# A fused attention and two-MLP kernel on one core: the first keys fetched and split per head, and three early steps issued behind the first scores

## The chip, the cores and the metric

One core of a Trainium2 chip. The metric is device microseconds of one execution; a comparison uses the median of several executions of either kernel. Engines are named as in the profile: PE (TensorE, matrix products; PEld its weight loads), DVE (VectorE), ACT (ScalarE), POOL (GpSimd), SP (SyncE, which here issues nearly all DMAs). SPq is SP's instruction queue.

## What is computed

```python
# attention, 2 x 8 heads, 576 rows, head size 64: only the 32 largest scores of a row count
scores = scale * q @ k.T
kth = np.partition(scores, -32, axis=-1)[..., -32:-31]
scores = np.where(scores >= kth, scores, -1e9)
x = softmax(scores) @ v                      # -> 1152 tokens x 512
# first MLP (float64 weights, 512 x 1536 twice and 1536 x 512)
xn = x / sqrt(mean(x * x) + 1e-6) * rms_g
x = (silu(xn @ w_gate) * (xn @ w_val)) @ w_out
# second MLP, routed: each token to the best of 8 experts, 512 x 1024 and 1024 x 512 each
out = gate_w * (relu(x @ w1[e]) @ w2[e])
```

## The kernel before, in words

The work runs in 36 attention pairs (9 tiles of 128 tokens, 4 pairs of heads each). A pair `p` is a query block, two heads `i`; `scores(p, i)` makes a row of 576 scores in two halves of 288 columns, each from two products on PE (rounded and residual part of the query), which ACT copies out (line 319). DVE then folds the two halves into larger and smaller ones (lines 324, 325) and `topk_folded` finds the 32 largest by rounds of "eight largest" (MAX8, lines 367, 376, 378, 379) and "strike them out" (line 373).

Before the products, keys and queries are split into a rounded part (ACT copy, lines 271 and 295) and a residual (a subtraction, lines 272 and 296, on DVE for pair 0 and on POOL later). The keys of two heads come as two DMAs of 64 partitions, one per partition half (`fetch_k`, line 266); the two partition halves are the two parts that one product contracts over, so a head's product needs both DMAs.

At the same time the weights of the first MLP are converted from float64 (`convert_all`): 12 units of 1 MB and 12 of 0.5 MB are fetched by `fetch` (line 137, always on SP), and `bits` makes 32-bit words of one: ACT rounds the low words (line 167), DVE joins them with the high ones (line 168) and sets the exponent (line 169). A gram product (line 193) and a few small steps find a power-of-two scale per block, whose last factor is the largest square of `rms_g` (lines 243 and `top`, lines 178 to 182), and `split` (lines 238 to 241) writes two half-precision parts. Only when all blocks are split can `moe1` of tile 0 start (lines 498 and 523), in which PE works off the first MLP tile by tile beside the attention of later tiles. The last 150 us are the routed MLP.

The order on each engine isn't written out: the code gives an order of issue (a list of slots, `at`, with priorities by `ahead`), and a scheduler then fixes one static order per engine from its own estimate of the times. Within an engine's order nothing overtakes. A new construct in the changed kernel, `tc.issue_after(x)`, keeps the instructions in its block from being placed ahead of `x`. Each DMA reports on one of eight landing semaphores, handed out in turn, and an issue waits until the previous DMA on its semaphore has landed.

The first instructions at the top of the program (lines 648 to 663): query 0, keys of pair 0, first weight unit, `rms_g`, query 1, keys of pair 1, two more units, then the splits and scores of pair 0, then the splits of pair 1.

Of the kernel before, what the change touches and what calls it, by code (L numbers as in the profile page):

```python
# [1 line left out]

# [6 lines left out]
F32 = mybir.dt.float32  # L9
# [4 lines left out]
U32 = mybir.dt.uint32  # L14
U8 = mybir.dt.uint8
AF = mybir.ActivationFunctionType
OP = mybir.AluOpType
PSUM = bass.MemoryType.PSUM

P = 128  # L20
B, H, S, D = 2, 8, 576, 64
N = B * S
DM = H * D
# [4 lines left out]
HALF = S // 2  # L28
KC = DM // P
# [14 lines left out]
LOW = 0.937  # L44


def tile_topk_attention__then__moe__then__moe_routed(
    tc: tile.TileContext,
    q_l, k_l, v_l, w_gate, w_val, w_out, rms_g, r_gate, w1, w2, capacity, out,
):  # L50
    args = (q_l, k_l, v_l, *(a.bitcast(I32) for a in (w_gate, w_val, w_out)), rms_g, r_gate, w1, w2, int(capacity), out)
    general, held, store = whole(tc, *args, False)
    with tc.If(general > W):
        whole(tc, *args, True)
        for to, _, _ in held[1:]:
            tc.nc.gpsimd.memset(to, int(NOWHERE))
    for x in held[1:]:
        store(*x)
    held[0].release()
# [3 lines left out]
def whole(  # L63
# [3 lines left out]
    nc = tc.nc  # L67
# [18 lines left out]
    gk = const.tile([P, KC], F32, name="gk")  # L86
    st = const.tile([P, 70], F32, name="st")
    inv, rinv, ga, g2 = st[:, 0:7], st[:, 7:14], st[:, 14:38].rearrange("p (b c) -> p b c", c=KC), st[:, 38:46]
# [18 lines left out]
    pm = tc.alloc_tile_pool(name="pm", bufs=3, space=PSUM)  # L107
# [10 lines left out]
    def staged(b, c):  # L118

        return 4 * b + 4 + c  # L120
# [1 line left out]
    def final(b, c):  # L122
        return 4 * b + c

    def fetch():
        n = coming[0]
        coming[0] += 1
        b, c, g = UNITS[n]
        r = slice(c * P, (c + g) * P)
        src = w_out[r, :] if b == 6 else (w_gate, w_val)[b % 2][r, (b // 2) * 2 * DM:(b // 2 + 1) * 2 * DM]  # L130
        if (b, c) in PLACE:
            at = PLACE[b, c]
            raw = wbig[:, at:at + 2 * g, :].bitcast(I32).rearrange("p (a two) f -> p a (two f)", two=2)
        else:
            raw = att.tile([P, g, 2 * DM], I32, name="wraw", bufs=4)
        wraw[n] = raw.rearrange("p a (f w) -> p a f w", w=2)
        nc.sync.dma_start(raw, src.rearrange("(a p) f -> p a f", p=P))

    def pow2_below_rsqrt(out, back, x, by, t):

# [12 lines left out]
    def convert_all():  # L153

        due = {}
        n = 0

        def later(k, f, *a):
            due.setdefault(n + k, []).append((f, a))

        def bits(n):
            b, c, g = UNITS[n]
            raw = wraw.pop(n)
            j = staged(b, c)
            a = wbig[:, j:j + g, :].bitcast(I32)
            low = raw[:, :, :, 0]
            nc.scalar.activation(low.bitcast(F32), low.bitcast(U32), AF.Copy, scale=-LOW * 2.0 ** -51, bias=-2.0)
            nc.vector.scalar_tensor_tensor(a, raw[:, :, :, 1], 3, low, op0=OP.logical_shift_left, op1=OP.bitwise_or)  # L168
            nc.vector.scalar_tensor_tensor(a, raw[:, :, :, 1], 0x3fffffff, a, op0=OP.bitwise_or, op1=OP.bitwise_and)  # L169
            while coming[0] < len(UNITS) and coming[0] <= n + (3, 4)[n >= 9]:  # L170
                fetch()
            if c + g == (NF1 if b == 6 else KC):
                later(1, gram, b)

        def top(out, x, row):

            m = route.tile([P, 8], F32, name="m8")
            nc.vector.max(m, x)
            d = mx.tile([P, ROW], F32, name="yd").bitcast(BF16)[:, :P]
            nc.scalar.activation(d, ident, AF.Copy, scale=m[:, 0:1])  # L180
            nc.tensor.matmul(row, ones16, d, start=True, stop=True)
            nc.vector.max(out, row)
# [57 lines left out]
            nc.tensor.matmul(t, negated, half(i, 0), start=False, stop=True)  # L240
            nc.scalar.activation(half(i, 1), t, AF.Copy)

        nc.vector.tensor_tensor(g2[:, 0:KC], gk, gk, op=OP.mult)
        top(g2, g2, pm.tile([P, DM], F32, name="pm")[:, :P])
        start, k = {}, 0
        for i, u in enumerate(UNITS):
            start[k] = i
# [1 line left out]
        while n < k or due:  # L249
            if n in start:  # L250
                bits(start[n])
            for f, a in due.pop(n, []):
                f(*a)
            n += 1
            yield
# [3 lines left out]

    raw = {}  # L260

    def fetch_k(b, hp):
        row = 12 * (hp % 2) if b == 0 else NW
        raw["k", b, hp] = wbig[:, row:row + 3, :].rearrange("p a f -> p (a f)")[:, :2 * S].rearrange("p (i s) -> p i s", i=2)
        for half in range(2):
            nc.sync.dma_start(raw["k", b, hp][64 * half:64 * half + 64], k_l[b, :, 2 * hp:2 * hp + 2, :])

    def split_k(b, hp, eng=nc.gpsimd):
        x = raw.pop(("k", b, hp))
        st = att.tile([P, 2, S], F32R, name="kst", bufs=6)  # L270
        nc.scalar.activation(st, x, AF.Copy)
        eng.tensor_tensor(st[64:], x[64:], st[64:].bitcast(F32), op=OP.subtract)
        kst[b, hp] = st

    def load_v(b, hp):
# [15 lines left out]
    def split_q(p, eng=nc.gpsimd):  # L291
        x = raw.pop(("q", p))
        qh[p] = att.tile([P, 2, P], F32R, name="qh", bufs=3)
        ql[p] = att.tile([P, 2, P], F32R, name="ql", bufs=3)
        nc.scalar.activation(qh[p], x, AF.Copy)
        eng.tensor_tensor(ql[p], x, qh[p].bitcast(F32), op=OP.subtract)

    def spans_of(t):
        lo, hi = t * P, t * P + P
        if hi <= S:  # L300
            return [(0, 0, P)]
        if lo >= S:
            return [(1, 0, P)]
        return [(0, 0, S - lo), (1, S - lo, P)]

    s_sb = {}

    hi, lo = {}, {}

    def scores(p, i):  # L310
        t, hp = divmod(p, 4)
        s = att.tile([P, S], F32, name="s", bufs=4)
        for c in range(2):
            sp = ps.tile([P, KC, P], F32, name="tp", bufs=3).rearrange("p a b -> p (a b)")[:, :HALF]
            for b, _, c1 in reversed(spans_of(t)):
                for n, x in enumerate((qh[p], ql[p])):
                    nc.tensor.matmul(sp[:c1], x[:, i, :c1], kst[b, hp][:, i, c * HALF:(c + 1) * HALF],  # L317
                                     start=(n == 0), stop=(n == 1))
            nc.scalar.activation(s[:, c * HALF:(c + 1) * HALF], sp, AF.Copy)  # L319
        s_sb[p, i] = s  # L320
        if not exact:
            r = att.tile([P, 2, HALF], F32, name="r", bufs=4)
            hi[p, i], lo[p, i] = r[:, 0], r[:, 1]
            nc.vector.tensor_tensor(hi[p, i], sp, s[:, :HALF], op=OP.max)  # L324
            nc.vector.tensor_tensor(lo[p, i], sp, s[:, :HALF], op=OP.min)  # L325

    def pair_scores(p):
        for i in range(2):
            scores(p, i)
# [317 lines left out]
    SL = 14  # L647
    fetch_q(0)
    fetch_k(0, 0)
    fetch()  # L650
    nc.sync.dma_start(gk, rms_g.rearrange("(c p) -> p c", p=P))
    fetch_q(1)
    fetch_k(0, 1)
    fetch()
    fetch()
    split_q(0, nc.vector)
    split_k(0, 0, nc.vector)
    scores(0, 0)
    scores(0, 1)
    split_q(1)  # L660
    split_k(0, 1)
    fetch_k(0, 2)
    load_v(0, 0)
    at(4, ahead(convert_all(), 300, 1000), 1.0)
    at(4, once(split_k, 0, 2))
    at(4, once(fetch_k, 0, 3))
    at(10, once(split_k, 0, 3))
# [21 lines left out]
    for p in range(NP):  # L689
        t, hp = divmod(p, 4)  # L690
# [343 lines left out]
    top = route.tile([P, 1], I32, name="top", bufs=1)  # L1034
# [76 lines left out]
```

## Time and profile before

| | |
|---|---|
| median of 3 executions | 672.41 us (672.27 to 673.39) |
| profiled execution | 673.78 us, of which the span from first to last instruction 672.0 us |
| busy in the span | PE 88%, DVE 79%, ACT 75%, POOL 54% |
| mean granted clock of PE | 0.97 of full speed |
| DMA | 80.05 MB, 119 GB/s over the span |

All times of the trace count from the start of the span; 1.8 us of the profiled execution lie outside it. A busy PE in this profile is not a PE at its peak, since its products are pipelined. An instruction's duration includes some 0.06 us to 0.1 us in which the next one has already started.

### The profile page before, as it was taken

What the parts mean: (1) busy time and instruction counts of PE and PEld (TensorE: products, weight loads), DVE (VectorE), ACT (ScalarE), POOL (GpSimd) and SP (SyncE); (2) the same over time, 40 slices, a digit from 0 to 9 for tenths busy, and PEclk for the clock granted to TensorE, in tenths of its full rate; (3) what the DMA queues carried; (4) which work ended last, traced back from release to release, by engine and by line L of the source; (5) the groups of instructions that cost most, each with busy time, mean ns of one, the idle gap of its engine ahead of it and who ended that gap; (6) DMA issues with size and microseconds to landing.
All of it is one profiled execution on the core that took longest, in us unless ns stands there. A gap on an engine that the chain in (4) does not pass through costs nothing.

```text
span 672.0 us, 13486 instructions
## 1 busy us (share of the span) xinstructions
PE 589.9 (88%) x4817; PEld 414.1 (62%) x4817; DVE 533.8 (79%) x1489; ACT 503.2 (75%) x978; POOL 364.1 (54%) x499
## 2 busy tenths in 40 slices
PE   1428878899998999999999999999798769999994
PEld 1314455446665667666676666665344669999994
DVE  3989999978899878888989899751647746999961
ACT  3469978996788798797878887876984519998721
POOL 2487554445569699778788796784614000132112
PEclk9999969899999999999999999999898779999998
DMA  8998256923000010001000000009300499999001
GB/s 234 260 349 283 105 195 228 275 52 79 14 13 33 12 48 29 13 10 31 17 25 17 9 25 1 1 19 362 153 1 19 154 193 388 322 349 354 27 22 41
DMA packets 47006, 80.05 MB, mean 119 GB/s; under 512 B 18716, under 2 KB 23324, under 8 KB 46930
## 3 DMA queue, kind: packets, MB, share of 16 engines
q1 hardware_dynamic: 43938, 74.02, 35.0%
q0 software_dynamic: 1792, 4.83, 1.9%
q8 instruction: 39, 0.64, 0.4%
q10 hardware_dynamic: 1200, 0.26, 0.2%
q14 instruction: 37, 0.30, 0.1%
HBM read 64.35 MB, written 12.27 MB: 114 GB/s over the span
## 4 chain that ended last, share of the span: by engine, by line
PE 48%; DVE 14%; ACT 12%; DMA 10%; POOL 7%; issue 6%; SPq 1%; POOLq 0%; ACTq 0%; DVEq 0%
PE pm L498 14%; PE pm L523 9%; PE xps L430 6%; PE acc L905 5%; PE tp L317 4%; PE tp L422 4%; DMA raw<-in_w_dram 3%; DVE split L819 2%; ACT junk L789 2%; DMA vt<-in_v_l_dram 2%; PE pm L238 2%; DVE wbig L168 1%; DVE wbig L169 1%; DMA gk<-in_rms_g_dram 1%; POOL pp L399 1%
## 5 line engine op out<-in xcount | busy, mean ns | idle before, releaser
L498 PE MATMUL pm<-wbig,xn 128*128 128x512 f16 x600 | 148.9, 382 | 0.1
L905 PEld LDWEIGHTS <-split 128*128 128x128 f16 x1728 | 117.9, 101 | 12.1 <-DMA xbT<-xb 5.9
L399 POOL TENSOR_TENSOR pp<-s,pp 128x576 f32<-128x576 f32 x72 | 102.0, 1433 | 18.0 <-ACT pp L398 17.6
L498 PEld LDWEIGHTS <-xn 128*128 128x128 f16 x648 | 62.8, 99 | 59.7 <-issue 2.0
L376 DVE MAX8 m<-r 128x8 f32<-128x288 f32 x216 | 96.2, 452 | 2.4
L373 DVE MATCH_REPLACE8 r<-m,r 128x288 f32<-128x288 f32 x216 | 95.1, 442 | 0.0
L317 PE MATMUL tp<-kst,qh 128*128 128x288 f32 (+1 forms) x160 | 64.4, 410 | 31.7 <-ACT s L319 14.4
L523 PE MATMUL pm<-wbig,hT 128*128 128x512 f16 x324 | 79.3, 386 | 1.6 <-ACT hT L468 1.4
L319 ACT ACTIVATE s<-tp 128x288 f32<-128x288 f32 x144 | 57.2, 416 | 13.4 <-PE tp L317 11.0
L819 DVE SCALAR_TENSOR_TENSOR split<-raw,sc,split 128x2048 f16<-128x2048 f32 (+1 forms) x32 | 65.7, 2078 | 0.1
L317 PEld LDWEIGHTS tp<-kst,qh 128*128 128x128 f32 (+1 forms) x160 | 31.3, 195 | 50.4 <-ACT s L319 21.8
L430 PE MATMUL xps<-pt,vt 128*64 128x128 f32 (+1 forms) x800 | 61.9, 275 | 0.0
L905 PE MATMUL acc<-hE,split 128*128 128x168 f16 (+2 forms) x864 | 59.0, 228 | 3.2 <-ACT junk L789 1.3
L422 PE MATMUL tp<-ident,pp 128*128 128x128 f32 x324 | 57.7, 288 | 4.1 <-DVE r L325 2.4
L905 PE MATMUL acc<-xgT,split 128*128 128x168 f16 (+1 forms) x768 | 59.2, 241 | 1.5 <-DMA xgT<-disp 1.5
L398 ACT ACTIVATE pp<-s,bias 128x576 f32<-128x576 f32 x72 | 52.0, 775 | 9.7 <-POOL bias L381 9.7
L404 ACT ACTIVATE pp<-pp,bias 128x576 f32<-128x576 f32 x72 | 56.9, 793 | 2.7 <-POOL pp L399 2.7
L423 ACT ACTIVATE pt<-tp 128x384 f32<-128x384 f32 x108 | 52.0, 500 | 9.2 <-PE tp L422 7.0
L789 ACT ACTIVATE junk<-raw 128x2048 bf16<-128x2048 f32 (+1 forms) x32 | 54.2, 1692 | 3.9 <-DMA raw<-in_w_dram 3.5
L324 DVE TENSOR_TENSOR r<-tp,s 128x288 f32<-128x288 f32 x72 | 32.5, 451 | 28.7 <-ACT s L319 28.2
L422 PEld LDWEIGHTS tp<-ident,pp 128*128 128x128 f32 x324 | 40.4, 145 | 21.9 <-DVE r L325 3.2
L430 PEld LDWEIGHTS xps<-pt,vt 128*64 128x64 f32 x800 | 44.5, 138 | 12.7 <-issue 11.1
(226 smaller groups left out, 1236.4 us busy)
## 6 DMA issues: line engine op xcount, KB each, us to landing
raw<-in_w_dram SPq DMA_DIRECT2D x28, 1024.0 KB, 9.1
wbig<-in_w_gate_dram SPq DMA_DIRECT2D x6, 1024.0 KB, 6.8
wbig<-in_w_val_dram SPq DMA_DIRECT2D x6, 1024.0 KB, 9.9
wraw<-in_w_out_dram SPq DMA_DIRECT2D x12, 512.0 KB, 5.9
disp<-wraw SPq DMA_DIRECT2D x18, 257.0 KB, 6.9
qraw<-in_q_l_dram SPq DMA_DIRECT2D x72, 64.0 KB, 2.3
wbig<-in_k_l_dram SPq DMA_DIRECT2D x16, 288.0 KB, 4.0
split<-in_w_dram SPq DMA_DIRECT2D x4, 1024.0 KB, 7.9
```

The source lines that it names most:

```text
L317: nc.tensor.matmul(sp[:c1], x[:, i, :c1], kst[b, hp][:, i, c * HALF:(c + 1) * HALF], start=(n == 0), stop=(n == 1))
L319: nc.scalar.activation(s[:, c * HALF:(c + 1) * HALF], sp, AF.Copy)
L373: nc.vector.match_replace(h[i], to[n - 1][:, i], h[i], -3.0e38)
L376: nc.vector.max(to[n][:, i], h[i])
L399: nc.gpsimd.tensor_tensor(w, s[i], w, op=OP.subtract)
L422: nc.tensor.transpose(tp[:, i, :], p2[:, o:o + P], ident)
L430: nc.tensor.matmul(xps[t][rows, hp, c0:c1], v, w, start=(n == 0), stop=(n == 4))
L498: nc.tensor.matmul(a, xn[:, x + c, :], half(i, lo), start=(c == 0 and n == 0), stop=(c == KC - 1 and n == 2))
L523: nc.tensor.matmul(yps, hT[f // KC][:, KC * hi + f % KC, :], half(i, lo), start=(f == 0 and n == 0), stop=(f == NF1 - 1 and n == 2))
L789: nc.scalar.activation(junk, raw[:, g * 2 * BIG // k:(g + 1) * 2 * BIG // k], AF.Square, accum_out=sc[:, 9 + g:10 + g])
L819: nc.vector.scalar_tensor_tensor(lo[:, r], raw[:, r], sc[:, 7:8], hi[:, r], op0=OP.mult, op1=OP.subtract)
L905: nc.tensor.matmul(a, u[:, c, col * P:(col + 1) * P], v[:, c, :a.shape[-1]], start=(c == 0 and n == 0), stop=(c == nk - 1 and n == 2))
```

## The change

Four edits, all in the program's first microseconds; everything else in the code is as before, and the scheduler's order follows from it.

1. The first weight unit is fetched on ACT's queue (`fetch(nc.scalar)`), no longer on SP behind the first keys.
2. The keys of pair 0 are fetched and split head by head: four DMAs of half the columns, two copies on ACT and two subtractions on DVE, each of half the size.
3. Query 1 and keys 1 are split only after the copies of both heads' scores of pair 0 have been placed on ACT; the first unit's rounding on ACT and its joining on DVE (lines 168 and 170 of the changed kernel) likewise stand behind those copies and behind the folds.
4. The square of `rms_g` moves from DVE to POOL (line 246), and its maximum is found behind the first unit's joining.

```diff
-    def fetch():
+    def fetch(eng=nc.sync):
...
-        nc.sync.dma_start(raw, src.rearrange("(a p) f -> p a f", p=P))
+        eng.dma_start(raw, src.rearrange("(a p) f -> p a f", p=P))
...
-            nc.scalar.activation(low.bitcast(F32), low.bitcast(U32), AF.Copy, scale=-LOW * 2.0 ** -51, bias=-2.0)
-            nc.vector.scalar_tensor_tensor(a, raw[:, :, :, 1], 3, low, op0=OP.logical_shift_left, op1=OP.bitwise_or)
+            with tc.issue_after(copied[0, 1].ins) if n == 0 and not exact else nullcontext():
+                nc.scalar.activation(low.bitcast(F32), low.bitcast(U32), AF.Copy, scale=-LOW * 2.0 ** -51, bias=-2.0)
+            with tc.issue_after(folded[0, 1].ins) if n == 0 and not exact else nullcontext():
+                joined.append(nc.vector.scalar_tensor_tensor(a, raw[:, :, :, 1], 3, low, op0=OP.logical_shift_left, op1=OP.bitwise_or))
...
-        nc.vector.tensor_tensor(g2[:, 0:KC], gk, gk, op=OP.mult)
-        top(g2, g2, pm.tile([P, DM], F32, name="pm")[:, :P])
+        def gains():
+            nc.gpsimd.tensor_tensor(g2[:, 0:KC], gk, gk, op=OP.mult)
+            with tc.issue_after(joined[0].ins):
+                top(g2, g2, pm.tile([P, DM], F32, name="pm")[:, :P])
+
+        later(3, gains)
...
+    def heads(b, hp):
+        return (0, 1) if b == 0 and hp == 0 else (slice(0, 2),)
...
-        for half in range(2):
-            nc.sync.dma_start(raw["k", b, hp][64 * half:64 * half + 64], k_l[b, :, 2 * hp:2 * hp + 2, :])
+        for i in heads(b, hp):
+            for half in range(2):
+                nc.sync.dma_start(raw["k", b, hp][64 * half:64 * half + 64, i], k_l[b, :, 2 * hp:2 * hp + 2, :][:, i])
...
-        nc.scalar.activation(st, x, AF.Copy)
-        eng.tensor_tensor(st[64:], x[64:], st[64:].bitcast(F32), op=OP.subtract)
+        for i in heads(b, hp):
+            nc.scalar.activation(st[:, i], x[:, i], AF.Copy)
+            eng.tensor_tensor(st[64:, i], x[64:, i], st[64:, i].bitcast(F32), op=OP.subtract)
...
-    fetch()
+    fetch(nc.scalar)
...
-    split_q(1)
-    split_k(0, 1)
+    with tc.issue_after(copied[0, 1].ins):
+        split_q(1)
+        split_k(0, 1)
```

SP's first DMAs. Before (`qraw` queries, `wbig<-in_k_l_dram` keys, `in_w_gate_dram` and `in_w_val_dram` weight units, `gk` is `rms_g`; DMAHW0 to DMAHW7 are the landing semaphores):

```order
L289 DMA qraw<-in_q_l_dram 64x256 x2
L266 DMA wbig<-in_k_l_dram 64x1152 x2
L137 DMA wbig<-in_w_gate_dram 128x2x1024
L651 DMA gk<-in_rms_g_dram 128x4x1
L289 DMA qraw<-in_q_l_dram 64x256 x2
L266 DMA wbig<-in_k_l_dram 64x1152 [waits DMAHW0_49]
L266 DMA wbig<-in_k_l_dram 64x1152 [waits DMAHW1_49]
L137 DMA wbig<-in_w_gate_dram 128x2x1024 [waits DMAHW2_49]
L137 DMA wbig<-in_w_val_dram 128x2x1024 [waits DMAHW3_49]
L266 DMA wbig<-in_k_l_dram 64x1152 [waits DMAHW4_49,Activation_49]
```

And now:

```order
L300 DMA qraw<-in_q_l_dram 64x256 x2
L276 DMA wbig<-in_k_l_dram 64x576 x4
L662 DMA gk<-in_rms_g_dram 128x4x1
L300 DMA qraw<-in_q_l_dram 64x256 [waits DMAHW0_49]
L300 DMA qraw<-in_q_l_dram 64x256 [waits DMAHW1_49]
L276 DMA wbig<-in_k_l_dram 64x1152 [waits DMAHW2_49]
L276 DMA wbig<-in_k_l_dram 64x1152 [waits DMAHW3_49]
L137 DMA wbig<-in_w_gate_dram 128x2x1024 [waits DMAHW4_49]
L137 DMA wbig<-in_w_val_dram 128x2x1024 [waits DMAHW5_49]
L276 DMA wbig<-in_k_l_dram 64x1152 [waits DMAHW6_49,Activation_49]
```

The first weight unit is gone from SP, and the second query's first DMA now waits on DMAHW0, which the first weight unit (on ACT's queue) now reports on; before, that unit reported on DMAHW4, and the third pair's keys waited for it.

ACT's first instructions. Before (`kst` split keys, `qh` split query, `yd` belongs to the maximum of `rms_g`, `s` scores):

```order
L295 ACTIVATE qh_121<-qraw_107 128x256 [waits DMAHW0_49]
L271 ACTIVATE kst_125<-wbig_87 128x1152 [waits DMAHW3_49,DMAHW2_49]
L167 ACTIVATE wbig_87<-wbig_87 128x1024 [waits DMAHW4_49]
L295 ACTIVATE qh_152<-qraw_114 128x256 [waits DMAHW7_49,DMAHW6_49]
L180 ACTIVATE yd_184<-ident_64,m8_182 128x128 [waits DVE_49,Pool_49]
L319 ACTIVATE s_128<-tp_129 128x288 [waits PE_49]
L319 ACTIVATE s_128<-tp_133 128x288 [waits PE_49]
L319 ACTIVATE s_140<-tp_141 128x288 [waits PE_49]
L271 ACTIVATE kst_156<-wbig_87 128x1152 [waits DMAHW1_49,DMAHW0_49]
```

And now:

```order
L137 DMA wbig_87<-in_w_gate_dram 128x2x1024
L306 ACT_TABLE_LOAD [waits DMAHW2_49]
L306 ACTIVATE qh_123<-qraw_107 128x256 [waits DMAHW1_49]
L282 ACTIVATE kst_127<-wbig_87 128x576 [waits DMAHW4_49,DMAHW3_49]
L282 ACTIVATE kst_127<-wbig_87 128x576 [waits DMAHW6_49,DMAHW5_49]
L330 ACTIVATE s_132<-tp_133 128x288 [waits PE_49]
...
L330 ACTIVATE s_144<-tp_149 128x288 [waits PE_49]
L306 ACTIVATE qh_156<-qraw_116 128x256 [waits DMAHW1_49,DMAHW0_49]
L282 ACTIVATE kst_160<-wbig_87 128x1152 [waits DMAHW3_49,DMAHW2_49]
L168 ACTIVATE wbig_87<-wbig_87 128x1024
L168 ACTIVATE wbig_87<-wbig_87 128x1024 [waits DMAHW4_49]
L182 ACTIVATE yd_224<-ident_64,m8_222 128x128 [waits DVE_49]
```

The score copies (four, two of them shown) no longer stand behind the first unit's rounding; that rounding now stands behind the copy of the second pair's keys.

DVE's first work after the constants. Before:

```order
L272 TENSOR_TENSOR kst<-wbig,kst 64x1152
L243 TENSOR_TENSOR st<-gk 128x4
L178 MAX m_182<-st 128x8
L168 SCALAR_TENSOR_TENSOR wbig<-wbig 128x1024
L182 MAX st<-pm 128x8
L324 TENSOR_TENSOR r<-tp,s 128x288
L325 TENSOR_TENSOR r<-tp,s 128x288
L169 SCALAR_TENSOR_TENSOR wbig<-wbig 128x1024
L367 MAX m<-r 128x8
```

And now:

```order
L283 TENSOR_TENSOR kst<-wbig,kst 64x576 x2
L335 TENSOR_TENSOR r<-tp,s 128x288
L336 TENSOR_TENSOR r<-tp,s 128x288
L378 MAX m<-r 128x8
...
L384 MATCH_REPLACE r<-m,r 128x288 x2
L170 SCALAR_TENSOR_TENSOR wbig<-wbig 128x1024
L180 MAX m_222<-st 128x8
L387 MAX m<-r 128x8 x2
L170 SCALAR_TENSOR_TENSOR wbig<-wbig 128x1024
L171 SCALAR_TENSOR_TENSOR wbig<-wbig 128x1024
```

Ten instructions of pair 0's scores (six in the gap) now come ahead of the first unit's joining, and the second unit's joining comes ahead of the first's exponent.

## Rows read from the trace of the kernel before

**Rows 1.** The page: engines' busy us; one group: busy us, mean ns | idle before.

```profile
PE 589.9 (88%) x4817; PEld 414.1 (62%) x4817; DVE 533.8 (79%) x1489; ACT 503.2 (75%) x978; POOL 364.1 (54%) x499
...
L319 ACT ACTIVATE s<-tp 128x288 f32<-128x288 f32 x144 | 57.2, 416 | 13.4 <-PE tp L317 11.0
```

**Rows 2.** Busy time by stretches: length, engines (instructions), granted PE clock, DMA share, GB/s.

```profile
100.00:110.00 10.00, 9.14 (x66) 5.82 (x65) 9.95 (x33) 10.00 (x23) 4.86 (x12) 1.00 0.37 120
...
140.00:150.00 10.00, 9.51 (x56) 5.09 (x55) 6.09 (x19) 10.00 (x25) 4.24 (x7) 1.00 0.27 69
...
300.00:350.00 50.00, 49.92 (x353) 32.39 (x351) 45.12 (x155) 40.10 (x96) 39.90 (x60) 1.00 0.07 20
```

**Rows 3.** Timeline of the first 20 us: start, us, instruction, idle before and its releaser.

```profile
0.73 1.22 SPq L289 DMA_DIRECT2D qraw<-in_q_l_dram  x2
...
1.99 1.24 SPq L266 DMA_DIRECT2D wbig<-in_k_l_dram  x2
...
3.26 0.59 SPq L137 DMA_DIRECT2D wbig<-in_w_gate_dram  x1
...
7.11 1.16 ACT L271 ACTIVATE kst<-wbig 128x1152 fp32r<-128x1152 f32 x1 [1.72 <-DMA wbig<-in_k_l_dram]
...
8.30 1.35 DVE L272 TENSOR_TENSOR kst<-wbig,kst 64x1152 fp32r<-64x1152 f32 x1 [2.46 <-ACT kst L271]
...
9.71 0.61 PE L317 MATMUL tp<-kst,qh 128*128 128x288 f32 x1 [9.71 <-DVE kst L272]
...
12.70 1.10 ACT L167 ACTIVATE wbig<-wbig 128x1024 f32<-128x1024 uint32 x1 [4.43 <-DMA wbig<-in_w_gate_dram]
...
13.08 0.16 DVE L243 TENSOR_TENSOR st<-gk 128x4 f32<-128x4 f32 x1 [3.43 <-DMA gk<-in_rms_g_dram]
...
13.83 1.23 DVE L168 SCALAR_TENSOR_TENSOR wbig<-wbig 128x1024 int32<-128x1024 int32 x1 [0.38 <-ACT wbig L167]
...
15.18 0.44 DVE L324 TENSOR_TENSOR r<-tp,s 128x288 f32<-128x288 f32 x1
15.54 0.45 DVE L325 TENSOR_TENSOR r<-tp,s 128x288 f32<-128x288 f32 x1
...
16.03 1.16 ACT L271 ACTIVATE kst<-wbig 128x1152 fp32r<-128x1152 f32 x1 [0.74 <-DMA wbig<-in_k_l_dram]
...
17.32 2.65 POOL L272 TENSOR_TENSOR kst<-wbig,kst 64x1152 fp32r<-64x1152 f32 x1 [1.67 <-ACT kst L271]
...
18.29 1.14 ACT L167 ACTIVATE wbig<-wbig 128x1024 f32<-128x1024 uint32 x1 [0.80 <-DMA wbig<-in_w_gate_dram]
...
19.46 1.59 DVE L168 SCALAR_TENSOR_TENSOR wbig<-wbig 128x1024 int32<-128x1024 int32 x1
...
20.02 0.61 PE L317 MATMUL tp<-kst,qh 128*128 128x288 f32 x1 [4.43 <-POOL kst L272]
```

**Rows 4.** Busy time by stretches of the start; the last two columns are DMA.

```profile
2.00:4.00 2.00, 0.00 (x0) 0.00 (x0) 0.00 (x0) 0.33 (x1) 1.34 (x7) 1.00 0.55 112
4.00:9.00 5.00, 0.00 (x0) 0.00 (x0) 1.12 (x2) 2.54 (x3) 0.00 (x0) 1.00 0.99 290
...
14.00:19.00 5.00, 1.12 (x3) 0.50 (x2) 4.97 (x11) 3.46 (x8) 3.09 (x2) 1.00 1.04 360
```

**Rows 5.** DMAs issued at 0.73, 1.99 and 7.80 us: count, size, us to landing.

```profile
qraw<-in_q_l_dram SPq DMA_DIRECT2D x1, 64.0 KB, 2.2
...
wbig<-in_k_l_dram SPq DMA_DIRECT2D x1, 288.0 KB, 3.8
...
wbig<-in_w_gate_dram SPq DMA_DIRECT2D x1, 1024.0 KB, 10.5
```

**Rows 6.** What SP's queue waited for, first 20 us: total, times, longest.

```profile
SPq L266 <- DMA wbig<-in_w_gate_dram: 3.7, 1, 3.7
```

**Rows 7.** What DVE waited for, first 60 us: total, times, longest.

```profile
DVE st L243 <- DMA gk<-in_rms_g_dram: 3.4, 1, 3.4
...
DVE wbig L168 <- POOL kst L272: 1.5, 1, 1.5
```

More of the change, by code (lines that the diff above doesn't have):

```diff
@@ L1 @@
-from contextlib import ExitStack
+from contextlib import ExitStack, nullcontext
 import concourse.bass as bass
@@ L306, in whole @@
     s_sb = {}
-    hi, lo = {}, {}
+    hi, lo, copied, folded, joined = {}, {}, {}, {}, []
     def scores(p, i):
@@ L318, in scores @@
                                      start=(n == 0), stop=(n == 1))
-            nc.scalar.activation(s[:, c * HALF:(c + 1) * HALF], sp, AF.Copy)
+            copied[p, i] = folded[p, i] = nc.scalar.activation(s[:, c * HALF:(c + 1) * HALF], sp, AF.Copy)
         s_sb[p, i] = s
@@ L324, in scores @@
             nc.vector.tensor_tensor(hi[p, i], sp, s[:, :HALF], op=OP.max)
-            nc.vector.tensor_tensor(lo[p, i], sp, s[:, :HALF], op=OP.min)
+            folded[p, i] = nc.vector.tensor_tensor(lo[p, i], sp, s[:, :HALF], op=OP.min)
     def pair_scores(p):
```

## The prediction

> **What bounds the kernel now.** I read the busy table first, then the busy times by stretch, then the timeline of the first 20 us, and last who waited for whom. Over the span PE is busiest, with 88% against DVE's 79% [rows 1], but that is a mean over stages. At 100 to 110 us DVE is busy 9.95 of 10 us and ACT 10.00; at 140 to 150 us DVE has fallen to 6.09 and ACT has 10.00; from 300 to 350 us PE has 49.92 of 50 [rows 2]. So the weight conversion with the first top-k rounds is DVE's and ACT's stage, and the tiles behind it are PE's. All four edits lie in the first 20 us. A microsecond of DVE saved there can reach the end, since DVE then works without a pause and PE takes over when the conversion is done.
>
> The reader should see two things in the first 20 us. DVE does nothing useful from the end of the key split (8.30 + 1.35 = 9.65) to 13.08, where it waits 3.4 for `rms_g` [rows 3, 7]; the first fold of scores starts only at 15.18, although the first product ran at 9.71, because ACT's score copies stand behind the rounding of the first weight unit, which landed at 12.70 [rows 3]. And the joining of the second unit at 19.46 follows straight on ACT's rounding of it (18.29 + 1.14 = 19.43), which itself waited 0.80 for the landing [rows 3]. At 19.46, then, it's a DMA and not DVE that is late. From 4 to 9 us the DMA engines are busy 0.99 with 290 GB/s, from 14 to 19 us 1.04 with 360 [rows 4].
>
> **What the change does, part by part.**
>
> *First head.* Its keys are half of what pair 0 fetched, 288 KB, and query 0 is two DMAs of 64 KB [rows 5]; beside them the first weight unit (1024 KB) now flows from the start. Without any sharing the head lands as today's first half of the keys does, of the same 288 KB: 1.99 + 3.8 = 5.8 [rows 3, 5]. If it must share so that all 1440 KB (1.47 MB) come first, it is 1.47 MB at 290 GB/s = 5.1 us from 2.0 us, where the first bytes flow: 7.1, and some tenths until the report. I take 7.3, near the upper end, because 290 GB/s was the rate with the engines already full [rows 4]. ACT's copy (1.16) and DVE's subtraction (1.35) fall to a little over half, say 0.65 and 0.75, so the first product starts at about 8.8 rather than 9.71 [rows 3].
>
> *Second head.* 288 KB more is 1.0 us: landing at 8.3, ACT and DVE done by 9.75. The four halves cost some 0.2 us more than the two wholes, in time when both engines were idle.
>
> *Folds.* The copies follow the products at once, so the first fold starts at about 10.2, not 15.18: two products of 0.61 that overlap [rows 3] end at 9.65 or so, a copy takes 0.42 [rows 1], and DVE is free at 9.75. That is 5 us earlier for pair 0. But DVE did other work in that time. What counts is how far DVE is at one point that both orders share: the joining of the second unit. Before it DVE spends 19.46 - 13.08 - 0.38 = 6.0 us [rows 3]. Now: ten instructions of pair 0 at 0.36 from start to start (15.18 to 15.54) to 0.44, say 3.9; the first unit's joining 1.2; the small maximum 0.1; two more of 0.4: again 6.0. The work is the same, so the gain at that point is 19.46 less the new start of the second unit's joining.
>
> *Second pair's keys.* SP's issue of query 1 now waits for the semaphore on which the first unit reports; call its landing W. That such a wait binds is seen today: the third pair's keys waited 3.7 us for this unit [rows 6]. From query 0's issue to the copy of pair 0's keys it took 7.11 - 0.73 = 6.4 [rows 3], and the same four DMAs follow W, so keys 1 land at W + 6.4. Today they were there at 16.03 [rows 3]. W lies between 0.73 + 1.3 (first bytes) + 1.05 MB at 290 GB/s (3.6) = 5.6, and today's whole time from issue to landing, 12.70 - 3.26 = 9.4, from 0.73: 10.2. With the 1.47 MB above it is 7.1 and some tenths: I take 7.7, hence 14.1 for keys 1.
>
> *First unit's rounding.* On ACT it now stands behind the copy of keys 1. That is 14.1 + 1.16, then 1.10: its joining starts at 16.4. DVE, which has its ten instructions done by 14.3 (10.2 + 3.9, and 0.2 of waiting for the second head), stands idle for 2.1 us. After that it is ready for the second unit at 16.4 + 1.2 + 0.1 + 0.8 = 18.5, a microsecond ahead of today.
>
> *Second unit.* SP issues it after W and four issues of 0.6, at 10.1 to 10.2, where it was 7.80. It can land at the earliest when keys 1 are in and 1.05 MB at 360 GB/s has followed, 14.1 + 2.9 = 17.0; if it takes today's 10.5 [rows 5], at 20.7. Both ends are one row away from the case, so I take the middle, 18.8; with rounding of 1.1 the joining starts at 19.9. That is 0.45 later than 19.46.
>
> *Small parts.* The square of `rms_g` leaves DVE (0.16) and lands on POOL, idle there until the key split of pair 1 at 17.32 [rows 3]. If that cover were gone it would delay pair 1 by what it takes. Pair 1's products start at 14.1 + 1.16 + 2.65 = 18.0, not 20.02, but ACT's copies of them stand behind the second unit's rounding, so little of the 2 us gets through.
>
> *Sum.* Against the profiled execution of 673.78 us (span 672.0 and 1.8 outside it; 1.4 above the median of 672.41): DVE +0.45 at the second unit, -0.16 for the square; today's later idle of 1.5 us on DVE, behind POOL's key splits [rows 7], can take up a lag as small as this; pair 0's and pair 1's rounds lie further ahead, worth perhaps 0.5. Together about -0.4: 673.4 for a profiled execution like this one, 672.0 for the median. The head start of 5 us is spent on waiting for the same bytes.
>
> **Rivals.**
>
> *The head start stays (faster).* If the first unit lands near its lower end, W = 5.6, keys 1 are there at 12.0 and the first joining can start at 14.3, without idle time. The second unit lands between 14.9 and 18.5, and its joining starts between 16.5 (DVE's own pace) and 19.6; in the middle, at 17.8, 1.7 us are gained, at best 3.0. That gives 669.4 to 670.7, say 670.2. For it: from 2 to 4 us the engines are busy only 0.55 [rows 4], room that the early unit fills. Against it: the keys want the same engines just then.
>
> *The early unit is in its own way (slower).* It shares the DMA engines with queries and keys, and SP stands still until it has landed. W = 10.2 gives keys 1 at 16.6, the first joining at 18.9, the second unit between 19.5 and 23.1 and its joining at 22.4: 2.9 us late, of which DVE's later idle of 1.5 may hide some. That is 673.8 to 675.3, say 674.6. By this working the new joining starts at W + 12.2, so the change breaks even at W = 7.3, and loses more than 0.2% above W = 8.6 where nothing is hidden. For it: the unit took 9.4 us today, much longer than its bytes need. Against it: part of that was queueing behind the keys.
> The Trainium skill, "DMA: Bandwidth & Descriptors", section "Issuing engines are not separate DMA queues", says that transfers started from different engines run on the same 16 DMA engines and interleave, so that a second issuer saves only issue time. By that rule W would lie at 7.1 or above, never at 5.6; no row here has two issuers at once in this stretch.
>
> *Another order further on.* The scheduler's order differs in many later places on every engine. PE, at 49.92 of 50 us [rows 2], has no time to lose or win there, but a wait of a microsecond at the change of stages is possible in either direction; it widens every case by about 1 us.
>
> **How the numbers follow.** A measurement of this kernel can tell about 0.2% (1.3 us) from no change. No change to speak of, at 672.0: 0.42. Head start kept, 670.2: 0.35. Early unit in its own way, 674.6: 0.23. With the spread of 1 us put on each, some of the faster case ends within 0.2% and some of the middle one outside: faster 0.36, same 0.40, slower 0.24. The likeliest case alone reaches from 670.8 to 673.4. The range that holds 8 in 10 takes in the faster case to its best end less a little, 668.8, and the slower one to its far end, 675.2.
>
> **What would show it.** In the changed profile: the first product near 8.8 and the first fold near 10.2; SP's issue of query 1 waiting for the first unit until about 7.7; ACT idle before the copy of keys 1 until about 14; DVE idle for some 2 us before the first joining; the second unit's joining near 19.9. I am wrong if that joining starts before 18 or after 21, or if it starts as forecast and the time still moves by over 0.2%: then the first 20 us don't decide, and a later stage does.

## The result and the profile after

| | before | after |
|---|---|---|
| median of 6 executions | 672.34 us (669.89 to 674.46) | 678.60 us (677.37 to 680.57) |
| ratio after to before | | 1.0089, 95% interval 1.0064 to 1.0115 |
| profiled execution | 673.78 us | 678.43 us |
| its span | 672.0 us | 676.6 us |

The change costs 6 us. I had forecast no change (672.0) and a range that ended at 675.2. The busy line of the page hardly differs from [rows 1]: PE 2.5 us more, DVE 6.4 us more.

```profile
PE 592.4 (88%) x4817; PEld 414.1 (61%) x4817; DVE 540.2 (80%) x1489; ACT 505.1 (75%) x979; POOL 373.7 (55%) x500
```

The first 20 us after, from the timeline, to be held against [rows 3]:

```profile
0.73 0.46 ACTq L137 DMA_DIRECT2D wbig<-in_w_gate_dram  x1
...
7.09 1.11 SPq L300 DMA_DIRECT2D qraw<-in_q_l_dram  x2
...
7.38 1.28 ACT L306 ACT_TABLE_LOAD   x1 [7.38 <-DMA qraw<-in_q_l_dram]
...
9.13 0.42 DVE L307 TENSOR_TENSOR ql<-qraw,qh 128x256 fp32r<-128x256 f32 x1 [7.13 <-ACT qh L306]
...
10.51 0.61 PE L328 MATMUL tp<-kst,qh 128*128 128x288 f32 x1 [10.51 <-DVE kst L283]
...
12.32 0.46 DVE L335 TENSOR_TENSOR r<-tp,s 128x288 f32<-128x288 f32 x1 [1.19 <-ACT s L330]
...
13.45 1.15 ACT L282 ACTIVATE kst<-wbig 128x1152 fp32r<-128x1152 f32 x1
...
14.50 1.12 ACT L168 ACTIVATE wbig<-wbig 128x1024 f32<-128x1024 uint32 x1
...
14.74 2.67 POOL L283 TENSOR_TENSOR kst<-wbig,kst 64x1152 fp32r<-64x1152 f32 x1 [0.38 <-POOL ql L307]
...
16.15 2.33 DVE L170 SCALAR_TENSOR_TENSOR wbig<-wbig 128x1024 int32<-128x1024 int32 x1
...
17.46 0.61 PE L328 MATMUL tp<-kst,qh 128*128 128x288 f32 x1 [4.66 <-POOL kst L283]
...
17.59 1.18 ACT L168 ACTIVATE wbig<-wbig 128x1024 f32<-128x1024 uint32 x1 [1.96 <-DMA wbig<-in_w_gate_dram]
...
19.21 1.20 DVE L170 SCALAR_TENSOR_TENSOR wbig<-wbig 128x1024 int32<-128x1024 int32 x1
```

Query 0 is ready on ACT only at 7.38, since its two DMAs now share the engines with the first unit (without the early unit, in run e7 below, it is ready at 3.62), so the first product is later than before (10.51, not 9.71). Still, pair 1's products start 2.6 us earlier (17.46, not 20.02), and the second unit's joining starts at 19.21 instead of 19.46. At 20 us the changed kernel is a quarter of a microsecond **ahead**.

It is behind when the first MLP starts. The products of `moe1` in the view of one line's instructions (first and last start; `late` is a second buffer for results of the same products), before:

```profile
L498 PE MATMUL pm<-wbig,xn x600: 376/379/634, 147.0 to 502.3; 128*128 128x512 f16 x150
L498 PE MATMUL late<-wbig,xn x48: 376/379/379, 487.8 to 507.3; 128*128 128x512 f16 x48
```

and after:

```profile
L509 PE MATMUL pm<-wbig,xn x600: 376/379/635, 152.8 to 507.6; 128*128 128x512 f16 x150
L509 PE MATMUL late<-wbig,xn x48: 376/379/380, 493.1 to 512.5; 128*128 128x512 f16 x48
```

From the first of these products to the last are 360.3 us before and 359.7 after. PE hardly pauses there (49.92 of the 50 us from 300 in [rows 2]), so the 5.8 us by which it starts late go nearly whole (4.6 us) to the end of the span.

So something between 20 and 147 us loses 6 us. Its clearest place is the last block, `w_out`, whose 48 gram products must be done before its scale and its splits. PE's gram products and DVE's last joinings in the timeline, before:

```profile
107.38 2.23 PE L193 MATMUL tp<-wbig 128*128 128x128 bf16 x36
...
113.51 0.78 PE L193 MATMUL tp<-wbig 128*128 128x128 bf16 x8
...
114.12 0.67 DVE L169 SCALAR_TENSOR_TENSOR wbig<-wraw,wbig 128x512 int32<-128x512 int32 x1
...
114.85 0.40 PE L193 MATMUL tp<-wbig 128*128 128x128 bf16 x4 [0.56 <-DVE wbig L169]
```

and after:

```profile
111.68 1.12 PE L240 MATMUL pm<-wbig,hT 128*128 128x512 f32 x2 [1.35 <-ACT wbig L243]
...
113.27 0.67 DVE L171 SCALAR_TENSOR_TENSOR wbig<-wraw,wbig 128x512 int32<-128x512 int32 x1
...
115.44 0.55 PE L433 MATMUL tp<-ident,pp 128*128 128x128 f32 x3 [1.77 <-DVE r L336]
...
116.50 2.37 PE L195 MATMUL tp<-wbig 128*128 128x128 bf16 x25 [0.51 <-ACT pt L434]
...
122.12 1.03 PE L195 MATMUL tp<-wbig 128*128 128x128 bf16 x15
...
123.31 0.29 PE L195 MATMUL tp<-wbig 128*128 128x128 bf16 x2
```

Before, 44 of the 48 are done when the last weights are joined (114.79), and the other four follow at once: 115.25. After, the weights are joined 0.85 us earlier, but in PE's order the products stand behind splits of earlier blocks that wait for ACT and behind transposes of a pair that wait for DVE, and attention's products stand between them: 123.6. That is 8.3 us late, with every byte there. How much of the 6 us this one place costs is for the runs to say. No edit touches this place: only the scheduler's order differs.

### The profile page after: what moved, and what is told of

It reads as the page before. It is cut to its first block, busy times and chain, and to the rows that moved or that the text cites. A ratio compares the mean times of both kernels' runs of the same rounds, so it can differ in the third digit from the quotient of the medians.

```text
span 676.6 us, 13487 instructions
## 1 busy us (share of the span) xinstructions
PE 592.4 (88%) x4817; PEld 414.1 (61%) x4817; DVE 540.2 (80%) x1489; ACT 505.1 (75%) x979; POOL 373.7 (55%) x500
## 4 chain that ended last, share of the span: by engine, by line
PE 50%; DMA 16%; ACT 10%; DVE 8%; issue 7%; POOL 6%; SPq 2%; POOLq 0%; ACTq 0%
PE pm L509 17%; PE pm L534 9%; PE xps L441 7%; DMA out_dram<-last,tos 7%; PE tp L328 5%; PE tp L433 4%; ACT junk L801 2%; DMA wbig<-in_k_l_dram 2%; DMA raw<-in_w_dram 2%; DVE wbig L171 2%; DMA disp<-wraw 2%; ACT split L826 2%; POOL pp L410 2%; PE pm L495 1%; PE pm L240 1%
## 5 line engine op out<-in xcount | busy, mean ns | idle before, releaser
L509 PE MATMUL pm<-wbig,xn 128*128 128x512 f16 x600 | 149.2, 382 | 0.1
L410 POOL TENSOR_TENSOR pp<-s,pp 128x576 f32<-128x576 f32 x72 | 104.3, 1465 | 10.7 <-ACT pp L409 10.0
L433 PE MATMUL tp<-ident,pp 128*128 128x128 f32 x324 | 55.8, 280 | 5.1 <-ACT pt L434 2.6
L240 PE MATMUL pm<-wbig,hT 128*128 128x512 f32 x72 | 44.4, 730 | 14.8 <-POOL hT L219 9.4
L433 PEld LDWEIGHTS tp<-ident,pp 128*128 128x128 f32 x324 | 39.0, 141 | 21.9 <-DVE r L336 3.9
L534 PEld LDWEIGHTS <-hT 128*128 128x128 f16 x324 | 30.3, 99 | 34.8 <-issue 2.9
```

Source lines behind the costliest of these rows:

```text
L410: nc.gpsimd.tensor_tensor(w, s[i], w, op=OP.subtract)
L433: nc.tensor.transpose(tp[:, i, :], p2[:, o:o + P], ident)
L509: nc.tensor.matmul(a, xn[:, x + c, :], half(i, lo), start=(c == 0 and n == 0), stop=(c == KC - 1 and n == 2))
L534: nc.tensor.matmul(yps, hT[f // KC][:, KC * hi + f % KC, :], half(i, lo), start=(f == 0 and n == 0), stop=(f == NF1 - 1 and n == 2))
```

## The experiments

**Theory 1**: the order that the scheduler made behind the front loses the time. **Theory 2**: the front's own work does (early unit, late query 0). **Theory 3**: one of the edits carries it whatever the order.

To part edits from order, the order is held. All instructions of the main part are named in a table, engine by engine, and chained in the issue order alone; nothing waits that didn't before:

```diff
+        for a, b in zip(names, names[1:]):
+            tc.add_manual_dep(known[b], a, mybir.DependencyInfo(mybir.DependencyClass.NoSync, mybir.DependencyReason.DATA), reason="pin")
...
     general, held, store = whole(tc, *args, False)
+    pin(tc, ORDER)
```

The table takes one kernel's own order up to some row of each engine and the other's behind it. All runs (start: first product of the first MLP, from the one profiled execution):

| run | edits | order | median us | ratio to before (95%) | start |
|---|---|---|---|---|---|
| e1 | all | new to 20 us, then old | 670.14 | 0.9965 (0.994 to 0.999) | 147.7 |
| e8 | all, e1 again | same | 671.51 | 0.9988 (0.9957 to 1.0018) | 148.0 |
| e5 | all | new to 43 us | 671.05 | 0.9964 (0.9939 to 0.999) | 145.5 |
| e6 | all | new to 65 us | 673.64 | 1.0014 (0.999 to 1.0038) | 149.2 |
| e2 | all | new to 97 us | 675.41 | 1.0039 (1.0013 to 1.0065) | 150.1 |
| e3 | all | new to 128 us | 676.77 | 1.0069 (1.0042 to 1.0096) | 153.3 |
| e4 | none | old to 20 us, then new | 680.78 | 1.0098 (1.006 to 1.0136) | 155.0 |
| e7 | all but 1 | as e1 | 670.05 | 0.9978 (0.9952 to 1.0004) | 146.3 |
| e16 | all | new, one swap on POOL | 676.81 | 1.0068 (1.0042 to 1.0094) | 150.7 |
| e9 | 1 | scheduled freely | 678.17 | 1.0067 (1.0038 to 1.0096) | 159.9 |
| e10 | 2 | scheduled freely | 669.24 | 0.9936 (0.9903 to 0.9968) | 147.5 |
| e18 | 2, e10 again | same | 669.28 | 0.9948 (0.9926 to 0.997) | 151.1 |
| e11 | 3 | scheduled freely | 678.96 | 1.0091 (1.0058 to 1.0124) | 153.8 |
| e12 | 4 | scheduled freely | 689.25 | 1.023 (1.0181 to 1.0279) | 152.5 |
| e13 | 4 | its own to 20 us, then old | 673.45 | 1.0 (0.9977 to 1.0024) | 144.8 |
| e14 | none | old to 20 us, then that of e12 | 687.48 | 1.0228 (1.0196 to 1.0261) | 154.3 |
| e15 | 2 | its own to 20 us, then old | 669.25 | 0.995 (0.9931 to 0.997) | 147.3 |
| e17 | none | old to 20 us, then that of e10 | 670.71 | 0.9977 (0.9959 to 0.9995) | 149.5 |

**Edits against order (e1 to e4).** The four differ in the table alone, e4 also in that it is the old code.

> All four edits of the change; the order of the first 20 us (17 products on PE, 24 instructions on DVE, 14 on ACT, 18 on POOL, 20 on SP) is that of the changed kernel, and everything behind them is held in the order of the kernel before. Theory 1 (the edits of the front cost next to nothing by themselves, and the 6 us are lost where the scheduler's order differs further on, between 97 and 128 us, where the 36 gram products of w_out stand on PE behind splits of earlier blocks): 671 to 673.5 us, as the kernel before. Theory 2 (the early unit, which holds query 0 back by 3.7 us and the first product by 0.8 us, costs the time, and the order behind it is indifferent): 677 to 680 us, as the changed kernel.

> None of the four edits; the first 20 us are in the order of the kernel before (17 products on PE, 22 instructions on DVE, 13 on ACT, 17 on POOL, 19 on SP), and everything behind them is held in the order of the changed kernel. Theory 1: 677 to 680 us, the loss without any of the edits. Theory 2: 671 to 674 us.

> All four edits; the order is that of the changed kernel up to about 97 us of its trace (222 products on PE, 165 instructions on DVE, 116 on ACT, 73 on POOL, 76 on SP) and that of the kernel before behind it. Theory 1: 671 to 674 us, since the 36 gram products of w_out stand again where the kernel before has them. Theory 2: 677 to 680 us. A third outcome, a loss that arises between 20 and 97 us: the first run of this group as before, this one at 677 or more.

> All four edits; the order is that of the changed kernel up to about 128 us of its trace (347 products on PE, 238 instructions on DVE, 167 on ACT, 103 on POOL, 111 on SP) and that of the kernel before behind it. Theory 1: 677 to 680 us, the whole loss, although the following 550 us are in the order of the kernel before. Theory 2: the same 677 to 680. Should it come out at 671 to 674, the loss arises behind 128 us, against both.

With the edits and the old order behind them the time isn't lost (0.9965); without any edit but in the new order it is (1.0098). Theory 2 falls. On the place I was wrong: with the new order up to 97 us, more than half of it is lost already (e2), not none. From 97 to 128 us, where the late gram products of `w_out` stand, it is about 0.3% (e3 against e2, and their intervals overlap). The granted clock of PE is a rival that the traces speak against: from 60 to 100 and from 100 to 150 us it is 0.87 and 0.97 before, 0.83 and 0.93 after, but e10, whose first MLP starts at 147.5, has 0.85 and 0.93. No run holds the kernel before in its own order, so what the chaining itself costs isn't measured; the nearest is e13, one small edit in the old order, at 1.0.

**Where the order loses (e5, e6, e8).**

> All four edits; the order is that of the changed kernel up to about 43 us of its trace (54 products on PE, 62 instructions on DVE, 31 on ACT, 31 on POOL, 41 on SP) and that of the kernel before behind it. The run with the new order up to 97 us lost some 5 us against the one with 20 us; this asks where between. Theory 1a (the loss arises where the softmax of a pair and the scale of a block interleave, from 65 us on: in the changed kernel two multiplications of the softmax on POOL stand inside the chain that finds a block's scale, and DVE waits 2.4 us for it at 72 us): 669 to 672.5 us. Theory 1b (it arises before 43 us, in the order of the first conversions): 674 to 677.

> All four edits; the order is that of the changed kernel up to about 65 us of its trace (127 products on PE, 102 instructions on DVE, 68 on ACT, 47 on POOL, 67 on SP) and that of the kernel before behind it. Theory 1a: 669 to 673 us, since the interleave of 70 to 74 us is again that of the kernel before. Theory 1b, or a loss between 43 and 65 us: 674 to 677.

> The kernel of the first run once more, beside these, to see whether its 0.35% are real: 0.994 to 0.999 of the kernel before if they are, within 0.002 of 1 if the first group favoured it by chance. Theory 1 and 2 as for the first run.

Up to 43 us the new order is as good as the old (0.9964), up to 65 us it has lost 0.5%, up to 97 us 0.75%, up to 128 us 1.05% against e5. e5 and e3 differ clear of noise; the steps between them (0.25% to 0.5%) are no larger than the intervals are wide. So the loss probably builds up, with no one wait behind it, through the stretch in which blocks are scaled and split between softmax steps. 1b (all before 43) falls by e5; e6, at 673.64, lies between the times that 1a and its rival gave, and doesn't decide whether something is lost before 70 us, as 1a denies. e8 leaves open how much of e1's 0.35% is real.

**One wait of it (e16).** In the changed kernel, POOL and DVE at 70 us in the timeline:

```profile
70.46 0.19 POOL L200 TENSOR_TENSOR m<-m,st 128x1 f32<-128x1 f32 x1
...
70.61 1.41 POOL L410 TENSOR_TENSOR pp<-s,pp 128x576 f32<-128x576 f32 x1
...
72.10 0.19 POOL L141 TENSOR_SCALAR m<-m 128x1 f32<-128x1 f32 x1
...
72.37 1.41 POOL L410 TENSOR_TENSOR pp<-s,pp 128x576 f32<-128x576 f32 x1
...
73.73 0.57 POOL L142 TENSOR_TENSOR m<-m,mhalf 128x1 f32<-128x1 f32 x1
...
74.33 0.15 DVE L148 TENSOR_SCALAR st<-m 128x1 int32<-128x1 int32 x1 [2.37 <-POOL m L142]
```

Two softmax multiplications of 1.41 us stand inside a chain of three tiny steps, and DVE stands behind its last. The busy times from 70 to 80 us (the columns of [rows 2]), before and after:

```profile
70.00:80.00 10.00, 7.88 (x39) 3.54 (x37) 9.97 (x20) 10.00 (x20) 6.75 (x6) 1.00 0.18 61
...
70.00:80.00 10.00, 8.96 (x28) 4.54 (x29) 7.53 (x19) 7.68 (x16) 7.50 (x11) 0.69 0.05 16
```

DVE, busy for 9.97 of the 10 us before, has 7.53 after. The swap, in POOL's order:

```diff
-L410 pp
 L141 m
-L410 pp
 L142 m
+L410 pp
+L410 pp
```

> The changed kernel, its order held, but for one swap on POOL near 70 us: the first factor and the power of a block's scale stand ahead of the two multiplications of a softmax instead of between and behind them. Theory 1a (DVE's 2.4 us wait for that power is a part of the loss): 675.5 to 677.5 us, and the wait gone from the trace. The rival (another engine is late there anyway, since the first product of the first MLP waits for the last splits on PE): 678 to 679.5 us, as the changed kernel.

The same stretch, swapped (lines are shifted by 1):

```profile
70.77 0.19 POOL L142 TENSOR_SCALAR m<-m 128x1 f32<-128x1 f32 x1
...
71.04 0.57 POOL L143 TENSOR_TENSOR m<-m,mhalf 128x1 f32<-128x1 f32 x1
...
71.58 2.77 POOL L411 TENSOR_TENSOR pp<-s,pp 128x576 f32<-128x576 f32 x2
...
71.91 0.14 DVE L149 TENSOR_SCALAR st<-m 128x1 int32<-128x1 int32 x1
```

The wait is gone. The MLP starts 2.1 us earlier (150.7, not 152.8), but that is one execution of each, and two of one kernel differ by more (147.5 in e10, 151.1 in e18). The median is 1.8 us lower and where theory 1a put it, but the interval overlaps that of the changed kernel, so the gain in time is likely rather than shown.

**The early unit (e7).**

```diff
-    fetch(nc.scalar)
+    fetch()
```

> The order of the first run (changed kernel for 20 us, then the kernel before), but the first weight unit fetched on SP behind the first keys, as before; three of the four edits are left. Theory 1 (what is gained or lost in the first 20 us hardly reaches the end): 669 to 672.5 us, within 2 us of the first run. Theory 2 (the early unit costs what it holds back): 2 us or more below the first run, with the first product near 8.5 us instead of 10.5. Where the early unit pays: 2 us or more above it.

ACT and PE in its timeline:

```profile
3.62 1.28 ACT L307 ACT_TABLE_LOAD   x1 [3.62 <-DMA qraw<-in_q_l_dram]
...
7.22 0.61 PE L329 MATMUL tp<-kst,qh 128*128 128x288 f32 x1 [7.22 <-DVE kst L284]
```

The first product comes 3.3 us earlier than with the early unit, and the time is that of e1 and e8 (0.9978 between 0.9965 and 0.9988). In this front the early unit neither pays nor costs anything that these runs can tell, which is some 0.25%.

**Each edit alone (e9 to e12).** The scheduler is free. The lines that are changed, in this order:

```diff
+    fetch(nc.scalar)
...
+        for i in heads(b, hp):
+            nc.scalar.activation(st[:, i], x[:, i], AF.Copy)
...
+    with tc.issue_after(copied[0, 1].ins):
+        split_q(1)
+        split_k(0, 1)
...
+            nc.gpsimd.tensor_tensor(g2[:, 0:KC], gk, gk, op=OP.mult)
+            with tc.issue_after(joined[0].ins):
```

e10 has the DMAs and subtractions per head too, e11 the two `issue_after` of the first unit.

> The kernel before with edit 1 alone (first weight unit on ACT's queue), scheduled freely. Theory 1 (any edit of the front reshuffles the order up to 150 us, and the time follows the start of the first MLP's first product, 1 us for 1 us; before 147.0 us, changed kernel 152.8): the time moves from the kernel before by what that product's start moves from 148.5 us, to within 1.5 us, whichever way; a move of 2 to 6 us by an edit worth less than 1 us in the held runs is well possible. Theory 3 (one of the four edits carries the loss whatever the order): one of these four runs at 677 to 680 us, the others within 1.5 us of the kernel before.

> The kernel before with edit 2 alone (keys of pair 0 fetched and split head by head), scheduled freely. Theories 1 and 3 as for the run with edit 1 alone.

> The kernel before with edit 3 alone (splits of pair 1 and the first unit's rounding and joining behind the first scores), scheduled freely. Theories 1 and 3 as for the run with edit 1 alone.

> The kernel before with edit 4 alone (square of rms_g on POOL, its maximum behind the first joining), scheduled freely; the moved work is 0.16 us and one product. Theory 1: even this one may move the time by microseconds, by where it puts the first MLP's first product. Theory 3 as for the run with edit 1 alone; by it this edit is worth nothing.

Three of four lose, one gains: theory 3 falls. Theory 1's finer rule, that the time follows the MLP's start, holds for e11 (5.3 us by its start, 5.4 measured, against the 673.53 of this group) and misses for the others: by its start e9 should lose 11.4 us and lost 4.6, e10 gain 1.0 and gained 4.3, e12 lose 4.0 and lost 15.7. (These count from 148.5, as the expectations do, though the profiled execution of the kernel before has 147.0; from there e11 should lose 6.8.) Nor do starts rank the runs that share the old order behind the front: e13 starts first of all (144.8) and is slower than e1 and e15. A start belongs to the one profiled execution, which can lie far from the median: 668.98 against 673.45 us in e13, 681.25 against 678.17 in e9. In e12 there is a second place, from 490 to 510 us. Busy times of that stretch in e12 (the columns of [rows 2]):

```profile
490.00:510.00 20.00, 15.19 (x69) 7.38 (x70) 12.67 (x27) 15.15 (x28) 10.43 (x10) 0.77 0.03 13
```

and before:

```profile
490.00:510.00 20.00, 20.00 (x116) 10.90 (x115) 13.18 (x39) 14.56 (x26) 2.58 (x3) 1.00 0.00 1
```

PE stands for a quarter of it where before it didn't stand at all, and its mean granted clock there is 0.77. The first MLP's products in e12:

```profile
L502 PE MATMUL pm<-wbig,xn x600: 376/379/634, 152.5 to 521.7; 128*128 128x512 f16 x150
L502 PE MATMUL late<-wbig,xn x48: 376/379/379, 507.7 to 528.1; 128*128 128x512 f16 x48
```

From the first to the last are 375.6 us, against 360.3 before; they start 5.5 us late, and 3.9 us are won back behind them. Most of e12's loss, then, arises in the very stretch in which PE seemed to have nothing to lose; I didn't follow each wait of it.

**Edit 4, order apart (e13, e14).** Orders held as above.

> Edit 4 alone, as in the run that took 689 us, in its own order for the first 20 us (11 products on PE, 22 instructions on DVE, 12 on ACT, 18 on POOL, 19 on SP) and the order of the kernel before behind them. Theory 1 (the 16 us are the order's): ratio to the kernel before 0.997 to 1.003, 671 to 675 us. The rival (the square on POOL or its later maximum costs them by itself, since every block's scale needs that maximum): 685 to 691 us.

> The kernel before, none of the edits, in its own order for the first 20 us and in the order that the scheduler made for edit 4 alone behind them. Theory 1: 683 to 691 us. The rival: 671 to 675 us.

The edit in the old order: 1.0. Its order without the edit: 1.0228, against 1.023 for both. An edit that moves 0.16 us of work and one small maximum changed the time by 15 us through the order alone. In e14, too, the first MLP's products take longer, 373.5 us from first to last (154.3 to 527.8), with the old code.

**Edit 2, order apart (e15, e17, e18).**

> Edit 2 alone, as in the run with ratio 0.9936, in its own order for the first 20 us (13 products on PE, 31 instructions on DVE, 14 on ACT, 17 on POOL, 22 on SP; first fold at 8.9 us instead of 15.2) and the order of the kernel before behind them. Theory 1 (a front that is ahead at 20 us hardly moves the end; the gain of edit 2 alone was mostly the luck of its order): 0.9965 to 1.0 of the kernel before. The rival (the earlier scores are the gain): 0.991 to 0.9955.

> The kernel before, none of the edits, in its own order for the first 20 us and in the order that the scheduler made for edit 2 alone behind them. If the 0.5% of edit 2 with the old order held are its earlier first scores: 0.997 to 1.003 of the kernel before (670.7 to 674.7 us). If the order made for it is the better one by itself: 0.991 to 0.996.

> Edit 2 alone, scheduled freely, once more: 0.990 to 0.997 of the kernel before if its gain is real, above 0.998 if the first group favoured it.

Here theory 1 fails on its other side. In the old order edit 2 still gains 0.5%. PE and DVE in its timeline (e15):

```profile
7.10 0.61 PE L323 MATMUL tp<-kst,qh 128*128 128x288 f32 x1 [7.10 <-DVE kst L278]
...
8.91 0.46 DVE L330 TENSOR_TENSOR r<-tp,s 128x288 f32<-128x288 f32 x1 [0.52 <-ACT s L325]
```

The first product starts 2.6 us earlier than before, the first fold 6.3 us. But how that reaches the end isn't shown. The first MLP of e15:

```profile
L504 PE MATMUL pm<-wbig,xn x600: 376/379/635, 147.3 to 504.6; 128*128 128x512 f16 x150
L504 PE MATMUL late<-wbig,xn x48: 377/379/380, 490.2 to 509.6; 128*128 128x512 f16 x48
```

It neither starts nor ends earlier than before (147.0 and 507.3). In the profiled executions the gain lies behind it: from the last of these products to the end of the span are 160.2 us in e15, 158.0 to 159.1 in e10, e17 and e18, and 164.7 before. But e1, e8 and e13, which gain less or nothing, have 159.7 to 161.9 there, so the kernel before may have been caught in a long execution. Edit 2 also adds two DMAs, which shifts the turn in which later ones take the landing semaphores; no run parts this from the earlier scores. The order made for edit 2 is worth 0.2% by itself on the old code (e17), but adds nothing clear of noise to the edit (e10 and e18 against e15). Edit 2 is the best version of the study, 669.24 and 669.28 us scheduled freely and 669.25 held, and it beats both kernels.

## Why the prediction was wrong

*First head.* Forecast 7.3 and a first product at 8.8; it came at 10.51. I shared the DMA engines between keys and first unit, but left query 0 at its old landing. It is the query that was held back, to 7.38 on ACT, and everything behind it; without the early unit the product starts at 7.22.

*Folds.* 12.32, not 10.2; 1.7 us of it is that same delay. Direction right, still 2.9 us earlier than before.

*Landing of the first unit, W.* 7.7 forecast. SP's issue of query 1, which waits for it, starts at 7.09. The Trainium skill, "DMA: Bandwidth & Descriptors", section "Issuing engines are not separate DMA queues", says that a second issuer's transfers run on the same engines as the first's; by the working of the prediction that puts W at 7.1 or above, and 7.09 agrees with it to the rounding.

*Second pair's keys, first rounding.* Keys forecast at 14.1; ACT copies them at 13.45 without a wait. The first joining starts at 16.15 (forecast 16.4), but DVE, late itself, is not idle for 2.1 us before it: ACT's rounding was done at 15.62, and DVE's own steps came last. That this forecast nearly fits is partly luck.

*Second unit.* 19.21, forecast 19.9, and 0.25 ahead of the kernel before instead of 0.45 behind. Inside the bounds that I had set for it, but by two misses that offset each other: the unit had landed by 17.59, not at 18.8, and its rounding was done at 18.77, while DVE came last, since the first joining took 2.33 us and not 1.2.

*Sum.* -0.4 us for the front; its terms as written (+0.45, -0.16, -0.5) give -0.2, and the rest is lag that the later idle was to take up. Held in the old order, the four edits are worth -2.3 and -0.8 us by their ratios in two groups, the second not clear of noise: right sign as far as that goes, small, and the range from 668.8 to 675.2 holds both medians.

*The early unit in its own way.* Half of its mechanism is there: query 0 comes 3.8 us later than in e7 (7.38 against 3.62). The other half isn't: SP stood only until 7.09, not until 10.2. At the end it costs nothing that e7 can show.

**The step that failed** is "another order further on", which I put at about 1 us in either direction because PE "has no time to lose or win there". I had read that from 300 to 350 us, where PE is at 49.92 of 50 [rows 2]. The order changed from 20 us on. From 50 to 140 us DVE, ACT and PE of the changed kernel are each busy between 5.9 and 10.0 of every 10 us, and hand each block's scale through POOL from one to the next between softmax steps; a tiny step that is queued behind a long one then stops the engine that waits for it, as DVE at 74.33. Measured, the new order costs 1.05% between 43 and 128 us (e3 against e5) and 1.0% over the whole program on the old code (e4, 6.6 us on the 672.46 of its group), and another, made for the smallest edit, 2.3%. Nor did the reading hold where I had made it: in e12 and e14 the first MLP, PE's own stage, takes 13 to 15 us longer. That the order is the cause is shown by the held runs; which waits make up the microseconds is shown for one place only. My second sign of being wrong named the case: the joining starts as forecast, the time moves, and a later stage decides.

Open: which waits behind 43 us add up to the 6 us; why all four edits in the old order gain 0.1% to 0.35% where edit 2 alone gains 0.5%, and by what path (edits 1 and 3 weren't tried held by themselves); and how far a start read from one execution can be trusted, since the same kernel had 147.5 in e10 and 151.1 in e18 with equal medians.

## What to carry to other kernels

Where a scheduler fixes the order from its own estimates, no edit is local: price the new order over the whole stage in which engines hand small results to each other, not only where the edit is, and give that term the largest spread. To learn what an edit is worth, run it once with the old order held behind it, and run the old code once in the new order; the two together parted 0.0% from 2.3% here. In such a stage look for short steps of a chain that stand behind long independent ones on the same engine; moving two of them ahead here removed a wait of 2.37 us, though the gain in time isn't clear of noise. And don't judge an order by where one stage starts in one execution.

## What the runs showed of the hardware

A joining on DVE, an operation on two tensors, took 1.20 us at 19.21 but 2.33 us at 16.15, while POOL subtracted keys from 14.74 to 17.41. POOL and DVE in the changed kernel's timeline at another such place; line 171 is the exponent step of a unit, 1.21 us at 68.05:

```profile
33.75 2.63 POOL L283 TENSOR_TENSOR kst<-wbig,kst 64x1152 fp32r<-64x1152 f32 x1 [4.26 <-ACT kst L282]
...
33.92 3.55 DVE L171 SCALAR_TENSOR_TENSOR wbig<-wbig 128x1024 int32<-128x1024 int32 x1
...
68.05 1.21 DVE L171 SCALAR_TENSOR_TENSOR wbig<-wbig 128x1024 int32<-128x1024 int32 x1
```

DVE's 3.55 us are its own 1.21 and the 2.46 us until POOL is done, to within 0.12, as if it stood still until then. I had put 1.2 for such a joining. The Trainium skill, "SBUF — State Buffer", section "Summary: rules for kernel authors", says the same: a DVE operation with two SBUF inputs and a GpSimd operation that reads SBUF exclude each other, and the second fully waits. Both numbers agree with it.
